# Useless matmuls in the head of an attention and gated-FFN kernel: another operand, another count, other places

## The chip, the cores and the metric

The kernel runs on one core of a Trainium2 chip. The metric is the device time of one execution in microseconds; the time given for a kernel is the median of its runs. A profiled execution gives the page and the trace that the text quotes; all its times count from the start of the core's span. TensorE is called PE there, VectorE DVE, ScalarE ACT, GpSimd POOL and SyncE SP; PEld is TensorE's loading of the stationary operand.

## The reference

Linear attention with a normalised output feeds a feed-forward layer with a sigmoid gate. All is float32 on the chip; the weights of the second part come in as 64-bit floats and are converted by hand.

```python
# q, k, v: (8 batches, 8 heads, 576 tokens, 64)
kv  = einsum('bhsd,bhse->bhde', k, v)
out = einsum('bhsd,bhde->bhse', q, kv)
rms = sqrt(mean(out * out, axis=-1, keepdims=True) + 1e-06)
x   = (out / rms * g_norm)            # then (B*S, H*D) = (4608, 512)
gate = 1 / (1 + exp(-(x @ w_gate)))   # w_gate, w_val: (512, 1536)
val  = x @ w_val
return (gate * val) @ w_out           # w_out: (1536, 512)
```

## The kernel before, in words

The 4608 tokens are taken in nine groups of 512. Group 0 runs through both layers of the feed-forward part in the plain way, 128x512 products at a time (line 618 for the first layer, 853 for the second). The eight other groups use a fast scheme of block products with sums formed ahead of them (lines 977 and 1079), and the attention of the later batches is done in between. All of that follows the head, and the change does not touch it.

The head is the stretch up to about 33 us. It does the attention of batch 0 alone, in four pairs of heads (n = 0 to 3), and converts the first two units of weights. Its order is written out by hand: a string of tokens (`order`, lines 651 to 656), which a loop (lines 658 to 673) turns into instructions one after the other. Each engine works off its own instructions in that order and waits on semaphores where it needs another's result. The tokens are these.

- `KVn` (line 299): 12 small products of k and v on TensorE; `KVOn` (303): VectorE copies the result out.
- `Qn` (309): six transposes of q on TensorE against the identity `ident`; `QOn` (314): ScalarE copies the result out.
- `Un` (326): 20 small products of q and kv; `SQn` (331): ScalarE squares them; `SUMn` (335): VectorE sums the squares; `ROOTn` (339): ScalarE takes the root; `NORMn` (343 and 345): VectorE takes the reciprocal and scales.
- `Xn` (353): five transposes of the scaled result, the second x being `X1`; `XOn` (362): ScalarE copies them into `xT`.
- `cu.i` and `au.i`: the steps of the conversion of weight unit u, the c steps on VectorE (lines 195, 210, 222, 226, 233) and the a steps on ScalarE (200, 215). Step `a0` adds the constant `one` as its bias.
- `b0.i.m` (618): products of the first block of the first layer; TensorE begins the second block after the head, when `c1.4` is done.
- `wu`: loads of weight unit u into a tile `st`.
- `warmN` (671): N products of no use, on the 128x128 tile `ident`, into a PSUM bank that is overwritten later. The profile counts each float32 product as two passes.

Loads of k, v and q for the four pairs go out on SyncE's queue ahead of all this (lines 93 and 100), the weight units in between (159). `ident` is made by GpSimd (a memset and a select in masks.py), and `one`, `exp_off` and `eps` by VectorE memsets (173, 175, 276). Tiles of one pool are placed in SBUF in the order in which they are made, so the size of `one`, the first of them, sets where the others begin.

Of the kernel before, what the change touches and what calls it, by code (L numbers as in the profile page):

```python
# [10 lines left out]
FP32 = mybir.dt.float32  # L11
# [9 lines left out]
def kernel(  # L21
# [11 lines left out]
    nc = tc.nc  # L33
# [4 lines left out]
    P = 128  # L38
# [34 lines left out]
    const = ctx.enter_context(tc.tile_pool(name="const", bufs=1))  # L73
# [75 lines left out]
    def load_unit(u, halves=(0, 1)):  # L149
        if u >= len(units):  # L150
            return
        kind, f = units[u]
        if 0 in halves:
            staged[u] = raw.tile([P, 2, DM], I64, tag="st", name="st", bufs=NST)
        st = staged[u]
        for i in halves:
            if kind == "gv":
                src = (moe_w_gate, moe_w_val)[i].rearrange("(m p) f -> p m f", p=P)[:, :, P * f:P * f + P]
                nc.sync.dma_start(out=st[:, i].rearrange("p (m f) -> p m f", m=NMT), in_=src)
            else:  # L160
                nc.sync.dma_start(out=st[:, i], in_=moe_w_out[P * (f + i):P * (f + i) + P, :])
# [7 lines left out]


    EXP_OFF = 896
    one = const.tile([P, 1], FP32, name="one")
    nc.vector.memset(one, 1.0)
    exp_off = const.tile([P, 1], FP32, name="exp_off")
    nc.vector.memset(exp_off, -EXP_OFF * 2.0 ** 23)

# [83 lines left out]
    w1 = const.tile([P, N3, 4 * NMT, 2, P], FP32, name="w1")  # L260
    w2 = const.tile([P, NFT, DM], FP32, name="w2")
    ident = const.tile([P, P], FP32, name="ident")
# [316 lines left out]
    def bank(i):  # L579
        return (psum_mm if i < 2 else psum).tile([P, 512], FP32, tag=f"mm{i}", name="mm")  # L580
# [19 lines left out]
    warm, pair_kv = bank(0), bank(1)  # L600
# [29 lines left out]
    def plain(c, u, ps, steps_at):  # L630
# [18 lines left out]


    order = """
        w1 w2 warm8 KV0 Q0 KVO0 QO0 warm4 U0 SQ0 KV1 Q1 SUM0 ROOT0 KVO1 QO1 NORM0 warm3 U1 SQ1 X0 XO0 SUM1 ROOT1
        c0.0 a0.0 c0.1 a0.1 NORM1 warm11 X1 XO1 c0.2 KV2 Q2 KVO2 QO2 c0.3 c0.4 w3 warm3 U2 SQ2 KV3 Q3 SUM2 ROOT2 KVO3 QO3
        NORM2 b0.0.0 U3 SQ3 b0.1.0 X2 XO2 c1.0 SUM3 ROOT3 a1.0 c1.1 a1.1 NORM3 b0.0.1 b0.1.1 b0.0.2 X3 XO3 b0.1.2
        c1.2 c1.3 c1.4 w4 b0.0.3 b0.1.3
    """
# [1 line left out]
    for token in order.split():  # L658
        name = token.rstrip("0123456789.")
        n = [int(i) for i in token[len(name):].split(".")]  # L660
        f = n[0]
        if name == "b":
            blk = blk or Plain(0, F_ORDER[0], (warm, pair_kv))
            blk.mm(n[1], n[2])
        elif name in ("c", "a"):
            conversion[f][name][n[1]]()
        elif name == "w":
            load_unit(f)
        elif name == "warm":
            for _ in range(f):  # L670
                nc.tensor.matmul(warm[:, 0:P], ident, ident, start=True, stop=True)
        else:
            a[f][steps[name]]()
            if token == f"Q{NE - 1}":
                first_ctx.__exit__(None, None, None)
                hp = ctx.enter_context(tc.tile_pool(name="hp", bufs=1))
                h_main = [hp.tile([P, 4 * NT, P], FP32, name=f"h{j}") for j in range(N3)]
                h_more = hp.tile([P, N3, 3 * NT, P], FP32, name="h_more")
# [469 lines left out]
    X1 = (18, 19, 20, 21, 22, 22, 23, 23, 24, 24, 25, 26, 28, 30, 31, 33, 35, 37)  # L1148
# [59 lines left out]
```

## Time and profile before

| what | value |
|---|---|
| median of 3 runs | 999.95 us (999.59 to 1000.1) |
| the profiled execution's own time | 1001.39 us |
| its span | 999.6 us |
| TensorE busy | 992.4 us, 99% of the span |
| VectorE, ScalarE, GpSimd busy | 719.1, 343.0, 616.2 us |
| first operation of TensorE | 1.37 us, the first of `warm8` |
| start of KV0, Q0, U0 | 5.08, 6.82, 9.70 us |
| start of U1, X1, U2 | 13.54, 18.38, 21.40 us |

The span runs from the core's first to its last instruction; the execution's own time has what lies around it as well. In the timeline a row names the start, the duration, the engine, the line, the operation, the tiles (out<-in), the shape and the number of instructions, and in brackets the idle time ahead of it and what ended it. In the chain of waits a row is a start, a duration and what the chain went through. Matmuls overlap, so a row's duration is somewhat longer than the distance to the next row's start.

### The profile page before, as it was taken

How to read it: one execution, taken by the hardware profiler on the slowest of the kernel's cores; microseconds unless marked ns; L12 is line 12 of the kernel's file. 1: busy time of each engine (PE TensorE's matmuls, PEld its weight loads, DVE VectorE, ACT ScalarE, POOL GpSimd, SP SyncE). 2: the span in 40 equal slices, each digit the busy share in tenths (PEclk: the TensorE clock that was granted, in tenths of full speed). 3: DMA queues.
4: the chain of work that ended last, by engine and by line, in shares of the span. 5: the costliest groups of instructions: out<-in, count | busy, mean ns of one | idle time of the engine just before them, and what ended most of it. 6: DMA issues, size and time to landing. Idle time of an engine off the chain costs nothing.

```text
span 999.6 us, 16578 instructions
## 1 busy us (share of the span) xinstructions
PE 992.4 (99%) x5958; PEld 816.2 (82%) x5958; DVE 719.1 (72%) x1185; ACT 343.0 (34%) x621; POOL 616.2 (62%) x991
## 2 busy tenths in 40 slices
PE   8999999999999999999999999999999999999998
PEld 7455447888888888888888888888888888888887
DVE  4989999898758766784777576866587566755672
ACT  4566332561144213530344124511442123213320
POOL 0439997798259634865286708771686349744963
PEclk9999999999999999999999999999999999999999
DMA  9995515763889468746975677656854455444614
GB/s 270 275 262 176 174 53 142 220 225 104 289 277 276 158 190 272 205 159 198 280 226 161 187 221 260 176 172 188 282 179 145 152 182 203 158 148 165 215 51 123
DMA packets 149522, 194.96 MB, mean 195 GB/s; under 512 B 79840, under 2 KB 121696, under 8 KB 149440
## 3 DMA queue, kind: packets, MB, share of 16 engines
q0 software_dynamic: 22512, 116.41, 35.1%
q1 hardware_dynamic: 120848, 75.66, 26.7%
q10 hardware_dynamic: 6080, 1.84, 0.8%
q8 instruction: 47, 0.77, 0.3%
q14 instruction: 35, 0.29, 0.1%
HBM read 160.04 MB, written 25.56 MB: 186 GB/s over the span
## 4 chain that ended last, share of the span: by engine, by line
PE 93%; DVE 4%; issue 1%; ACT 1%; DMA 0%; SPq 0%; DVEq 0%; ACTq 0%
PE mm L977 54%; PE mm L1079 27%; PE mm L618 5%; PE mm L853 3%; PE at L450 2%; DVE cz L226 1%; DVE w L222 1%; DVE w L195 1%; PE at L400 1%; PE mm L400 1%; DVE cz L210 0%; DMA q<-in_q_dram 0%; PE two L326 0%; DVE w L235 0%; DVE h L626 0%
## 5 line engine op out<-in xcount | busy, mean ns | idle before, releaser
L977 PE MATMUL mm<-xs,w 128*128 128x256 f32 x1428 | 331.8, 380 | 0.0
L977 PEld LDWEIGHTS mm<-xs,w 128*128 128x128 f32 x1428 | 270.5, 190 | 37.9 <-ACT sg L943 1.2
L977 PE MATMUL mm<-xT,w 128*128 128x256 f32 x948 | 230.6, 380 | 0.0
L977 PEld LDWEIGHTS mm<-xT,w 128*128 128x128 f32 x948 | 179.5, 190 | 25.0 <-issue 0.5
L799 POOL DMA_DIRECT2D w<-kept x84 | 46.9, 559 | 203.6 <-PE mm L977 200.1
L947 DVE TENSOR_TENSOR sg<-sg,mm 128x512 f32<-128x512 f32 (+1 forms) x176 | 100.8, 599 | 75.1 <-PE mm L977 34.4
L1079 PE MATMUL mm<-w,h 128*128 128x256 f32 x630 | 142.8, 379 | 0.0
L1079 PEld LDWEIGHTS mm<-w,h 128*128 128x128 f32 x630 | 119.7, 190 | 16.3
L943 ACT COPY temps<-mm 128x512 f32<-128x512 f32 (+1 forms) x128 | 66.2, 540 | 184.7 <-PE mm L1079 94.7
L939 POOL TENSOR_TENSOR h<-h,sg 128x512 f32<-128x512 f32 x72 | 96.8, 1362 | 43.9 <-ACT sg L936 27.8
L752 POOL TENSOR_TENSOR h<-h 128x128 f32<-128x128 f32 x216 | 109.9, 521 | 16.6 <-DVE h_more L752 13.1
L1079 PE MATMUL mm<-w,h_more 128*128 128x256 f32 x474 | 108.2, 379 | 0.0
L936 ACT ACTIVATE sg<-sg 128x512 f32<-128x512 f32 x96 | 59.7, 630 | 127.3 <-DVE sg L947 127.3
L1079 PEld LDWEIGHTS mm<-w,h_more 128*128 128x128 f32 x474 | 90.1, 190 | 12.2
L943 ACT COPY sg<-mm 128x512 f32<-128x512 f32 (+1 forms) x112 | 56.5, 511 | 84.1 <-PE mm L1079 45.3
L752 POOL TENSOR_TENSOR h_more<-h 128x128 f32<-128x128 f32 x120 | 58.5, 491 | 34.8 <-DVE h L939 30.5
L947 DVE TENSOR_TENSOR temps<-temps,mm 128x512 f32<-128x512 f32 (+1 forms) x96 | 59.5, 620 | 27.1 <-PE mm L1079 16.8
L947 DVE TENSOR_TENSOR temps<-mm,temps 128x512 f32<-128x512 f32 (+1 forms) x64 | 39.8, 623 | 52.3 <-PE mm L1079 23.9
L618 PE MATMUL mm<-xT,w 128*128 128x512 f32 x176 | 77.2, 595 | 0.1
L943 ACT COPY h<-mm 128x512 f32<-128x512 f32 x48 | 28.1, 586 | 142.9 <-PE mm L977 142.9
L947 DVE TENSOR_TENSOR sg<-mm,sg 128x512 f32<-128x512 f32 (+1 forms) x64 | 39.7, 620 | 42.4 <-PE mm L1079 21.9
L618 PEld LDWEIGHTS mm<-xT,w 128*128 128x128 f32 x176 | 32.8, 190 | 40.0 <-issue 36.8
(154 smaller groups left out, 1298.1 us busy)
## 6 DMA issues: line engine op xcount, KB each, us to landing
w<-kept POOLq DMA_DIRECT2D x42, 896.0 KB, 5.1
w<-kept POOLq DMA_DIRECT2D x90, 384.0 KB, 4.5
w<-kept POOLq DMA_DIRECT2D x42, 768.0 KB, 5.0
out_dram<-sg SPq DMA_DIRECT2D x119, 64.0 KB, 1.7
q<-in_q_dram SPq DMA_DIRECT2D x96, 72.0 KB, 5.1
xT<-xTs SPq DMA_DIRECT2D x96, 72.0 KB, 4.6
st<-in_moe_w_gate_dram SPq DMA_DIRECT2D x12, 512.0 KB, 5.3
st<-in_moe_w_val_dram SPq DMA_DIRECT2D x12, 512.0 KB, 6.6
```

The lines of the kernel that those rows point to most:

```text
L400: nc.tensor.matmul(ps[m][HD * g:HD * g + HD, e], mains[2 * m + g, "k"][:, c], mains[2 * m + g, "v"][:, c], start=(b == 2 and e == 0 and j ...
L450: nc.tensor.matmul(to[HD * e:HD * e + HD], qTs[HD * g:HD * g + HD, c:c + HD], kvq[HD * g:HD * g + HD, m, e], start=True, stop=True)
L618: nc.tensor.matmul(self.ps[i], w[("wg", "wv")[i], self.f][:, m, :], xT[self.c][:, m, :], start=(m == 0), stop=(m == NMT - 1), skip_group_c ...
L752: ops.append((eng, lambda v=v, x=x, sign=sign, y=y, eng=eng: eng.tensor_tensor(out=h_form(v, j), in0=h_form(x, j), in1=h_form(y, j), op=op ...
L799: nc.gpsimd.dma_start(out=granule(g)[:, 0:n], in_=kept1[g // NPA % N3, g % NPA][:, 0:n])
L853: nc.tensor.matmul(ps[t], gv[0, f][:, P * t:P * t + P], w["wo", f], start=(f == 0), stop=(f == NFT - 1), skip_group_check=True)
L936: nc.scalar.activation(out=o["o" + step[1]], in_=o["o" + step[1]], func=AF.Sigmoid)
L939: mult.tensor_tensor(out=o[x], in0=o[x], in1=o[y], op=ALU.mult)
L943: nc.scalar.copy(out=o[out_], in_=o[expr])
L947: tt(out=o[out_], in0=o[x], in1=o[y], op=ALU.add if sign == "+" else ALU.subtract)
L977: nc.tensor.matmul(regions[name][1][:, g], ws[:, g], xf[c][wv], start=(new and g == 0), stop=True, skip_group_check=True)
L1079: nc.tensor.matmul(regions[name][1], h_form(hv, j), ws[:, j], start=(used[i] and j == 0), stop=(j == N3 - 1), skip_group_check=True)
```

## The change

A tile of ones, 128x128, takes the place of the 128x1 constant `one`, which becomes its first column; one VectorE memset sets it. The useless products multiply this tile with itself in place of `ident`. Their counts and places change: `warm8` becomes `warm9`; a `warm1` is new between KV0 and Q0; `warm4` ahead of U0 becomes `warm3`; a `warm1` is new between U0 (with SQ0) and KV1; `warm11` ahead of X1 becomes `warm14`. In all that is five products more (from 29 to 34).

```diff
-    one = const.tile([P, 1], FP32, name="one")
-    nc.vector.memset(one, 1.0)
+    ones = const.tile([P, P], FP32, name="ones")
+    nc.vector.memset(ones, 1.0)
+    one = ones[:, 0:1]
...
     order = """
-        w1 w2 warm8 KV0 Q0 KVO0 QO0 warm4 U0 SQ0 KV1 Q1 SUM0 ROOT0 KVO1 QO1 NORM0 warm3 U1 SQ1 X0 XO0 SUM1 ROOT1
-        c0.0 a0.0 c0.1 a0.1 NORM1 warm11 X1 XO1 c0.2 KV2 Q2 KVO2 QO2 c0.3 c0.4 w3 warm3 U2 SQ2 KV3 Q3 SUM2 ROOT2 KVO3 QO3
+        w1 w2 warm9 KV0 warm1 Q0 KVO0 QO0 warm3 U0 SQ0 warm1 KV1 Q1 SUM0 ROOT0 KVO1 QO1 NORM0 warm3 U1 SQ1 X0 XO0 SUM1 ROOT1
+        c0.0 a0.0 c0.1 a0.1 NORM1 warm14 X1 XO1 c0.2 KV2 Q2 KVO2 QO2 c0.3 c0.4 w3 warm3 U2 SQ2 KV3 Q3 SUM2 ROOT2 KVO3 QO3
...
-                nc.tensor.matmul(warm[:, 0:P], ident, ident, start=True, stop=True)
+                nc.tensor.matmul(warm[:, 0:P], ones, ones, start=True, stop=True)
```

## The prediction

> **What bounds the kernel now.** I read the page first, then the chain of waits in order of time, then TensorE's timeline over the head, and last the waits of TensorE after the head.
>
> ```profile
> PE 992.4 (99%) x5958; PEld 816.2 (82%) x5958; DVE 719.1 (72%) x1185; ACT 343.0 (34%) x621; POOL 616.2 (62%) x991
> PE   8999999999999999999999999999999999999998
> ```
>
> TensorE is busy for 99% of the span, and the only slices below 9 are the first and the last. The waits of TensorE from 34 us on hold no row at all. So the end of the run is the end of the head plus a fixed sum of matmuls plus a fixed tail: whatever the head gives up or gains by 33.13 us, when block 1 of the first layer begins, reaches the end unshortened. The question is only how many of the first 33 us the change moves.
>
> The chain of waits, in order of time, shows what sets the head (start, duration, what):
>
> ```profile
> 2.44 4.25 DMA q<-in_q_dram
> 6.68 0.14 issue
> 6.82 1.19 PE two L309 x6
> 8.01 1.76 PE mm L671 x8
> 9.77 1.27 PE two L326 x40
> 11.05 0.02 issue
> 11.07 0.71 ACT sqs L331
> ```
>
> The first q lands at 6.68, its transposes (Q0) follow, then the four useless products of L671 stand on the chain with 1.76 us, then U0. After that the chain alternates between ScalarE, VectorE and TensorE up to the second weight unit's conversion (c1.4), whose last operation ends at 32.98; TensorE begins block 1 at 33.13.
>
> TensorE's own timeline (start, duration, instruction, in brackets the idle time before it):
>
> ```profile
> 1.37 3.78 PE L671 MATMUL mm<-ident 128*128 128x128 f32 x16 [1.37 <-POOL ident masks.py:199]
> 5.08 1.55 PE L299 MATMUL mm<-v,k 96*64 96x64 f32 x24
> 6.82 1.19 PE L309 MATMUL two<-ident,q 96*128 96x96 f32 x6 [0.19 <-DMA q<-in_q_dram]
> 7.80 1.97 PE L671 MATMUL mm<-ident 128*128 128x128 f32 x8
> 9.70 1.29 PE L326 MATMUL two<-kvq,qTs 64*64 64x64 f32 x40
> 10.93 0.92 PE L299 MATMUL mm<-v,k 96*64 96x64 f32 x24
> 11.78 0.71 PE L309 MATMUL two<-ident,q 96*128 96x96 f32 x6
> 13.54 0.81 PE L326 MATMUL two<-kvq,qTs 64*64 64x64 f32 x40 [0.35 <-ACT qTs L314]
> 14.89 2.62 PE L671 MATMUL mm<-ident 128*128 128x128 f32 x22
> 18.38 0.73 PE L353 MATMUL two<-ident,sqs 128*128 128x128 f32 x5 [0.87 <-DVE sqs L345]
> ```
>
> The same work has two prices. A pass of L671 (each product is two passes) costs 3.78/16 = 0.236 us at first and 2.62/22 = 0.119 later; KV costs 1.55 against 0.92, Q 1.19 against 0.71, U 1.29 against 0.81. The page's clock row rounds this away, but the array runs at half rate until some moment inside U0: its first groups still start at the slow distance, its last at the fast one, which puts the rise at about 10.7. TensorE had by then worked since 1.37 with one stop: after KV0, at 6.63, it waits 0.19 us for q. The 5.26 us of unbroken work ahead of that stop did not raise the clock; the 3.9 us after it did.
>
> [...]
>
> **The change, part by part.** TensorE gets two rows more (850 to 852); no other engine's order changes, nor any DMA's.
>
> Start. The operand is now `ones`, one VectorE memset at 0.81, where before two GpSimd operations ended at 1.31. VectorE's memset of 128x1 takes 0.06 and GpSimd's of 128x128 takes 0.20; so `ones` is ready between 0.87 and 1.01, TensorE follows 0.05 later, and begins 0.30 to 0.45 us sooner. I take 0.35, near the 128x128 row. The two small memsets behind it on VectorE slip by up to 0.15, and their readers come far later (ScalarE's first activation at 3.29).
>
> warm9. One product more: 2 x 0.236 = 0.47. KV0 starts at 5.08 - 0.35 + 0.47 = 5.20 (its v has landed at 4.82) and ends at 6.75.
>
> The first new warm1 takes 0.47, so Q0 starts at about 7.2, not 6.82. That is +0.4 on the chain, and TensorE no longer stops there. warm3 in place of warm4 gives 0.47 back. With the slow clock all through: Q0 to about 8.2, three products (6 x 0.236 = 1.4) to 9.6, U0 at 9.6 against 9.70: a gain of 0.1, no more.
>
> The second warm1 costs 2 x 0.119 = 0.24 ahead of KV1. It is hidden: Q1 ends at 12.49 and ScalarE copies it only at 12.87, behind ROOT0, so 0.38 us of cover. Without that cover it would cost 0.24.
>
> warm14. Three products more, 6 x 0.119 = 0.71, in the 0.87 us in which TensorE waits for VectorE's NORM1 ahead of the second x: hidden with 0.16 to spare. Uncovered it would cost up to 0.7.
>
> What the filled wait does to the clock is shown by no row of before, so I bound it. Lower end: nothing, the gain of 0.1. Upper end: the clock is up before Q0. Then Q0 waits for its data (6.82 as now) and takes 0.6 of TensorE's time, not 1.0; ScalarE copies it 0.25 after that for 0.64, and U0 starts at 8.3, not 9.70 (1.4 sooner), taking 0.81, not 1.29 (0.5): 1.9 in all. Between them: TensorE now works unbroken from about 1.02, so 5.26 us of it are over at 6.3 and the rise should come somewhere from there on. With a rise during Q0 (7.2 to 7.8) Q0 ends at 7.8, the copy at 8.7, U0 starts 1.0 sooner and takes 0.5 less: 1.5.
>
> What is late next: after U0 the chain is engine on engine, so 1.5 is passed on until the second weight unit's data, which land at 23.95. Its first conversion step (c1.0) starts at 25.26 now, so this can move by 1.2 at most; the steps behind it wait for ScalarE and move by the full 1.5, and the gap closes to some 0.1 to 0.2. Everything else in the head (q2 at 17.56, v3 at 19.68, q3 at 20.49) lands before its moved use. I take 1.35.
>
> The sum against the profiled execution: it took 1001.39 (span 999.6 and 1.8 around it), and 1001.39 - 1.35 = 1000.04. The timed runs have a median of 999.95, 1.44 below the profiled one. If that is what profiling costs, the changed kernel takes 999.95 - 1.35 = 998.6; bounds 998.05 (1.9) and 999.85 (0.1).
>
> Addresses. `one` was 4 bytes per partition and `ones` is 512, so nearly every tile allocated after it moves up by 480 bytes: q, k, v, h and xT, which began on multiples of 256 bytes, begin 224 past one. I cost that at nothing. On TensorE, L977's passes lie 216 ns apart with xT as with the weight ring, which already begins 224 past; on the queues, the weight units' packets of 1024 bytes, written into `st`, which begins 224 past, take 46 ns, in line with the 18 ns of a 256-byte packet into the aligned q tiles.
>
> **The rivals.**
>
> First, the timed runs already have the early rise. The 1.44 us by which they beat the profiled run is about what the early rise is worth (1.35 to 1.9). If the moment of the rise depends on where the first matmul falls, the profiled run was the unlucky one, and the change has 0 to 0.3 left to give: 999.8. For it: 1.44 fits; against it: three runs within 0.5 us of each other, and profiling may well cost this much. [...]
>
> Second, the change doesn't do what it says: the stop of 0.19 us is not what held the clock. Q0's six transposes, 1.0 us at the slow rate, lay across the same place, and stay there. Then the rise stays at about 10.7 and the result is -0.1 to +0.3: 1000.0. [...]
>
> Third, slower: the shifted addresses split packets. In the head the DMA engines are the pace (busy share 0.9 and above from 3 to 30 us). If each of the 4608 q packets (256 bytes) and 1536 k and v packets of the head pays a second packet's fixed cost of some 9 ns (a packet of 128 bytes takes 13 ns and one of 256 takes 18, which leaves 8 or 9 for one without data), that is 6144 x 9 / 16 = 3.5 us more ahead of the second weight unit. It lands at 27.4 in place of 23.95, c1.0 starts 2.2 later, and the run takes 1002.2. It decides from 1.3 us of added DMA time on, the slack of c1.0 today. Against it: the 46 ns above, at the same offset. [...] The `st` rows do not agree with a visible cost.
>
> Fourth, more than forecast: if the timed runs rise even later than the profiled one, after 14 us, U0, KV1, Q1 and U1 all ran slow, about 1.1 us more than in the profile, and the change brings 1.9 + 1.1 = 3.0: 997.0. For it speaks only the narrow spread of the timed runs.
>
> **How the numbers follow.** A measurement of this kernel can tell about 0.2%, that is 2.0 us, from no change. Forecast (rise before or in Q0, against timed runs that rise late): 0.42, at 998.6, of which 0.10 lies beyond 2.0 us, since its upper end of 1.9 is worked from rounded rows. Timed runs already early: 0.30, at 999.8. Rise unmoved: 0.13, at 1000.0. Packets split, or another delay of that size: 0.07, at 1002.2. A still later rise in the timed runs: 0.08, at 997.0. So faster by over 0.2%: 0.10 + 0.08 = 0.18; slower: 0.07; within: 0.75. The range 997.9 to 1000.3 takes in the first three cases but for the edge of the forecast, and leaves out the last two: about 8 in 10.
>
> **What would show it.** In the profile after: L671 starting near 1.0; no idle bracket at Q0 (L309); Q0 at about 7.2 with later passes at the fast distance; U0 at 8.7 or sooner and at 0.81 us, not 1.29; the second x still waiting for VectorE, with a wait of 0.1 to 0.3, not 0.87; block 1 at about 31.8, not 33.13; and a span near 998.2. The forecast is wrong if U0 stays near 9.6 at 1.29 us, if the second x waits for TensorE's own products, or if q or the weight units land later than now.

## The result: 6 us slower, and what the profile after shows

| | changed kernel | kernel before |
|---|---|---|
| median of the timed runs | 1006.08 us (1005.14 to 1008.99, 6 runs) | 1000.03 us |
| ratio | 1.0062, 95% interval 1.005 to 1.0074 | 1 |
| the profiled execution's own time, span | 1006.25, 1004.5 us | 1001.39, 999.6 us |

The forecast was 998.6 us, with a range up to 1000.3. One of the six runs of the kernel before took 3718.28 us; the ratio goes by the others. A second measurement of the changed kernel, on record as a0_after_again, gave 1007.07 us, ratio 1.0066 (1.0051 to 1.0081).

The page of the changed kernel, busy time of each engine and TensorE's row in 40 slices:

```profile
PE 993.4 (99%) x5968; PEld 816.2 (81%) x5968; DVE 718.1 (71%) x1185; ACT 343.0 (34%) x621; POOL 614.8 (61%) x991
PE   9989999999999999999999999999999999999998
```

TensorE has ten passes more and 1.0 us more busy time, but the span is 4.9 us longer: the loss is waiting. The new 8 is the third slice, about 50 to 75 us, far behind the last instruction that the diff touches.

TensorE's timeline over the head of the changed kernel (start, duration, instruction, in brackets the idle time before it):

```profile
1.06 4.21 PE L672 MATMUL mm<-ones 128*128 128x128 f32 x18 [1.06 <-DVE eps L277]
5.20 1.55 PE L300 MATMUL mm<-v,k 96*64 96x64 f32 x24
6.68 0.71 PE L672 MATMUL mm<-ones 128*128 128x128 f32 x2
7.22 0.66 PE L310 MATMUL two<-ident,q 96*128 96x96 f32 x6
7.72 0.86 PE L672 MATMUL mm<-ones 128*128 128x128 f32 x6
8.61 0.81 PE L327 MATMUL two<-kvq,qTs 64*64 64x64 f32 x40
13.41 3.29 PE L672 MATMUL mm<-ones 128*128 128x128 f32 x28
16.90 0.74 PE L354 MATMUL two<-ident,sqs 128*128 128x128 f32 x5 [0.20 <-DVE sqs L346]
22.22 0.69 PE L310 MATMUL two<-ident,q 96*128 96x96 f32 x6 [0.63 <-DMA q<-in_q_dram]
```

What the forecast said of the first half of the head is there: the start at 1.06, Q0 at 7.22 without a wait and at the fast rate, U0 at 8.61 and 0.81 us long, the second x waiting only 0.20. The clock rose at 7.17 (10.81 before), and X1 starts 1.48 us sooner. From there on the gain shrinks: Q3 waits 0.63 for q, and block 1 begins at 32.23, 0.90 sooner than before and not 1.35. The first conversion step of the second weight unit (c1.0), on VectorE, shows where that went; the first line is the changed kernel, the second the kernel before:

```profile
25.28 0.69 DVE L196 TENSOR_SCALAR w<-st 128x1024 uint32<-128x1024 uint32 x1 [1.41 <-DMA st<-in_moe_w_val_dram]
25.25 0.77 DVE L195 TENSOR_SCALAR w<-st 128x1024 uint32<-128x1024 uint32 x1
```

The step waits 1.41 us for its weights, and starts no sooner than before. The chain of waits of the changed kernel, in order of time (start, duration, what), goes through transfers where before it went from engine to engine (an excerpt):

```profile
6.24 7.28 DMA st<-in_moe_w_val_dram
13.51 0.02 issue
13.53 8.55 DMA q<-in_q_dram
22.08 0.14 issue
22.22 0.69 PE two L310 x6
```

Behind the head no wait of TensorE over 0.15 us stood in the trace before. The waits of TensorE of the changed kernel from 33 us on (engine, line, what ended the waits: us in total, times, longest):

```profile
PE mm L978 <- issue: 2.0, 2, 1.5
PE at L451 <- ACT kvq L414: 1.6, 1, 1.6
PE mm L619 <- issue: 1.1, 1, 1.1
PE mm L854 <- DVE w L236: 0.4, 2, 0.2
```

They are of two kinds: waits for data that hang on a load, and waits put down to "issue", where TensorE waited for nothing that the profile shows. The DMA issues of both pages (tile, kernel, queue, count, size, median us from issue to landing) show the loads. Before:

```profile
q<-in_q_dram SPq DMA_DIRECT2D x96, 72.0 KB, 5.1
st<-in_moe_w_gate_dram SPq DMA_DIRECT2D x12, 512.0 KB, 5.3
st<-in_moe_w_val_dram SPq DMA_DIRECT2D x12, 512.0 KB, 6.6
```

After:

```profile
q<-in_q_dram SPq DMA_DIRECT2D x96, 72.0 KB, 6.0
st<-in_moe_w_gate_dram SPq DMA_DIRECT2D x12, 512.0 KB, 7.3
st<-in_moe_w_val_dram SPq DMA_DIRECT2D x12, 512.0 KB, 7.6
```

The bytes and the packets are the same. In the packet records of the first 24 us, a 256-byte packet into q takes 23.4 ns on the mean (18.8 before) and one of 1536 bytes into k and v 93.7 (84.7). These are the tiles that begin 224 bytes past a multiple of 256 since the tile of ones grew. The first difference is clear of what varies between runs: the kernels below whose q tiles are aligned have 18.6 to 19.7, those with shifted ones 23.4 to 25.4. For the 1536-byte packets the spans come close, 84.7 to 90.7 against 92.5 to 102.8.

### The profile page after: what moved, and what is told of

Its sections match the earlier page's. It is cut to its first block, busy times and chain, and to the rows that moved or that the text cites. A ratio compares the mean times of both kernels' runs of the same rounds, so it can differ in the third digit from the quotient of the medians.

```text
span 1004.5 us, 16598 instructions
## 1 busy us (share of the span) xinstructions
PE 993.4 (99%) x5968; PEld 816.2 (81%) x5968; DVE 718.1 (71%) x1185; ACT 343.0 (34%) x621; POOL 614.8 (61%) x991
## 4 chain that ended last, share of the span: by engine, by line
PE 89%; DVE 5%; DMA 3%; issue 1%; SPq 1%; ACT 0%; DVEq 0%
PE mm L978 54%; PE mm L1080 27%; PE mm L854 3%; PE mm L619 2%; PE at L451 2%; DMA st<-in_moe_w_val_dram 1%; DVE cz L227 1%; DVE w L223 1%; DMA q<-in_q_dram 1%; DMA h_more<-in_v_dram 1%; DVE w L196 1%; SPq L132 1%; PE at L401 1%; PE mm L401 1%; DVE cz L211 0%
## 5 line engine op out<-in xcount | busy, mean ns | idle before, releaser
L978 PE MATMUL mm<-xs,w 128*128 128x256 f32 x1428 | 331.9, 380 | 1.5 <-issue 1.5
L978 PEld LDWEIGHTS mm<-xs,w 128*128 128x128 f32 x1428 | 270.5, 190 | 39.6 <-issue 1.7
L978 PE MATMUL mm<-xT,w 128*128 128x256 f32 x948 | 230.8, 380 | 0.5 <-issue 0.5
L978 PEld LDWEIGHTS mm<-xT,w 128*128 128x128 f32 x948 | 179.5, 190 | 25.7 <-issue 1.2
```

What stands on the lines that cost most here:

```text
L978: nc.tensor.matmul(regions[name][1][:, g], ws[:, g], xf[c][wv], start=(new and g == 0), stop=True, skip_group_check=True)
```

## The experiments

Two numbers of each trace order all runs: the start of block 1, which ends the head, and the time from there to TensorE's last instruction, which before was 995.73 - 33.13 = 962.60 us. "Added" counts TensorE's instructions against before: the five products more are 20, as each is two passes and each pass a weight load and a product.

| kernel | big tiles past a multiple of 256 B | added | median us | ratio (95%) | block 1 | from block 1 on |
|---|---|---|---|---|---|---|
| before | 0 | 0 | 1000.03 | 1 | 33.13 | 962.60 |
| changed | 224 | 20 | 1006.08 | 1.0062 (1.005, 1.0074) | 32.23 | 968.35 |
| a0_after_again | 224 | 20 | 1007.07 | 1.0066 (1.0051, 1.0081) | 33.87 | 967.20 |
| e1_after_512 | 0 | 20 | 1000.77 | 1.0006 (0.9997, 1.0015) | 31.31 | 964.79 |
| e2_before_480 | 224 | 0 | 1002.11 | 1.0016 (1.0007, 1.0025) | 33.68 | 963.67 |
| e5_order_alone | 0 | 20 | 1000.29 | 0.9999 (0.999, 1.0008) | 31.64 | 963.22 |
| e4_first_h_aligned | 0 where loads of k, v, q, h land; others 224 | 20 | 1000.98 | 1.0006 (0.9997, 1.0015) | 31.91 | 964.59 |
| e6_512_warm9 | 0 | 0 | 1000.10 | 0.9999 (0.9987, 1.0011) | 31.52 | 962.60 |
| e9_512_h_off | 0, but h 224 | 20 | 1004.66 | 1.0046 (1.0028, 1.0063) | 31.69 | 965.74 |
| e10_480_h_on | 224, but h 0 | 20 | 1002.74 | 1.0019 (1.001, 1.0029) | 36.63 | 963.19 |
| e7_off64 | 64 | 20 | 1005.70 | 1.0044 (1.003, 1.0057) | 32.28 | 967.52 |
| e11_all_256 | 0, `st` too | 0 | 999.54 | 0.9986 (0.9977, 0.9994) | 31.27 | 962.58 |
| e12_before_warm16 | 0 | 20 | 1001.39 | 1.0003 (0.9994, 1.0012) | 33.16 | 963.12 |
| e13_480_warm9 | 224 | 0 | 1001.87 | 1.002 (1.0011, 1.0029) | 32.21 | 963.60 |
| e14_before_all_256 | 0, `st` too | 0 | 999.67 | 0.9998 (0.9989, 1.0006) | 31.37 | 962.06 |

Each ratio is to runs of the kernel before on the same chip, and not to the 1000.03 of the first row; e1, e2, e4 and e5 shared theirs, as did a0, e6, e9 and e10, then e7, e11 and e12, then e13 and e14. e2, e12 and e14 have the order of before; all others have the new order (e6, e11 and e13 with nine products ahead of the second x), and of these e5 starts at 1.37 as before, since it keeps the identity tile. The two columns on the right are of one profiled execution each.

### Order or addresses

e1_after_512, the changed kernel with the tile of ones 32 bytes larger, so that all later tiles stand on multiples of 256 again:

```diff
-    ones = const.tile([P, P], FP32, name="ones")
+    ones = const.tile([P, P + 8], FP32, name="ones")[:, 0:P]
```

> The changed kernel, with the tile of ones 544 bytes long per partition in place of 512 (the products still read its first 128 columns). Every later tile then lies 512 bytes above its place in the kernel before, not 480, so q, k, v, h and xT begin on multiples of 256 again; the order and the products are those of the changed kernel. Address theory (packets that begin off a 256-byte boundary take longer, and the loads of the head and of h_more come late): the loss of 6 us goes and the earlier clock stays, 0.9 to 1.9 us under the kernel before, 998.1 to 999.1. Timing theory (the earlier head makes the SyncE and GpSimd loads collide, whatever the addresses): about 1006. In the trace the 256-byte packets of the head average 18.8 ns by the address theory, 23 by the other.

e2_before_480, the kernel before with the 512-byte tile alone:

```diff
-    one = const.tile([P, 1], FP32, name="one")
+    one = const.tile([P, P], FP32, name="one")[:, 0:1]
```

> The kernel before, with the tile `one` 512 bytes long per partition; only its first column is set and used. Order and products are those of before, all later tiles move up by 480 bytes. Address theory: the packets slow down as in the changed kernel (256-byte ones from 18.8 to 23 ns on average), q3 lands after 21.5 in place of 20.5, TensorE stops for h_more near 60 us, and the run takes 1004 to 1008. Timing theory: no change, 999.6 to 1000.3.

e5_order_alone, the kernel before with the new `order` string and nothing else:

> Only the new counts and places of the useless products, still on the identity and at the old addresses, so they begin at 1.37 as before. [...] Timing theory: slower, 1003 to 1006, as far as the head still ends sooner.

e4_first_h_aligned, the changed kernel with 32 bytes more ahead of the tiles that k, v, q and the later tiles of the pool `hp` (h and `h_more`) are loaded into; `xT`, `xTs` and the late q tiles stay at 224:

```diff
+    sb.tile([P, 8], FP32, name="pad", bufs=1)
```

> The changed kernel with 32 bytes of padding behind the tiles that live through the whole kernel, so that the head's k, v, q and the later h and h_more begin on multiples of 256 again, while xT, xTs and the late q tile stay 224 past one. Address theory: if the loads of the head and of h_more make the loss near 60 us, that stop goes and q3 lands near 20.5; what the late q loads (128-byte packets) and the writes to xT lose stays, 999 to 1004. If all of the loss is in the head and h_more: 998.5 to 999.5. Timing theory: about 1006.

Thirty-two bytes of padding take back all but some 0.6 of the 6 us (e1), and so does aligning only the tiles that loads of the head and of batch 1 go into (e4). The new order alone costs nothing that can be told from no change (e5). The gain of 0.9 to 1.9 us that was expected of e1, and of 0.5 to 1.5 of e5, did not come. So the address does it, but not alone: with the order of before the same shift costs 1.6 us (e2), a quarter of the loss and not the 4 to 8 us that were expected.

a0_after_again, the changed kernel once more beside the runs that follow:

> The changed kernel itself once more, on the chip of the parts, so that they can be compared with it. Both theories: 1005 to 1007, with the stop of about 2 us ahead of the head's successor near 61 us and stops of 0.7 and 1.6 us near 506 and 719.

It gave 1007.07 us, with the waits at the same places (1.2 us for `kvq`, stops of 1.3 and 1.1 us; the one near 720 us is 0.1). Its profiled execution spreads the loss otherwise than the first: the clock is up at 5.16, but Q0, Q1 and Q3 wait 0.55, 0.67 and 0.46 us for q and the second x 1.34, and block 1 begins at 33.87, later than before.

### What the five added products have to do with it

In the profile after, the waits put down to "issue" end at 64.63, 506.17 and 719.62 us. Counted through the trace, these are TensorE's instructions number 1217, 6593 and 9409 (weight loads, products and semaphore instructions together, counted from 0), all of them 193 more than a multiple of 256. One of the DMA queues that the page calls "instruction" moves packets of 16 KB, one of which starts 2.4 us ahead of each stop's end: at 62.24, 503.72 and 717.21. The page has 47 packets in that queue, and the trace 12203 instructions of TensorE, 260 to a packet; the stops lie 5376 = 21 x 256 and 2816 = 11 x 256 instructions apart. From these numbers it is estimated that a packet brings a block of 256 of TensorE's instructions; no record names what a packet holds.

e6_512_warm9 is e1 with nine products in the last changed place and not fourteen, so that TensorE issues as many instructions as before:

```diff
-        c0.0 a0.0 c0.1 a0.1 NORM1 warm14 X1 XO1 ...
+        c0.0 a0.0 c0.1 a0.1 NORM1 warm9 X1 XO1 ...
```

> The changed kernel at aligned addresses (tile of ones 544 bytes), and with nine useless products ahead of the second x in place of fourteen, so that TensorE has as many instructions in the head as the kernel before. Theory of instruction fetch (the stops near 503 and 715 us fall on the same TensorE instructions, 6593 and 9409, whatever the time, 11 x 256 apart; they are blocks of instructions that arrive late): the block ends return to where they lie in the kernel before, and the two stops, 0.27 and 0.51 us, go: 0.3 to 0.8 under the aligned kernel with fourteen, 999.8 to 1000.4. Rival (the stops are waits for data that the earlier head brings about): they stay at the same work. In both, the second x waits 0.6 us longer on TensorE without a loss, as VectorE ends that wait.

No stop was left at any of the three, and from 33 us on TensorE has no wait over 0.15 us. From block 1 to the end it took 962.60 us, the same as before to the hundredth. e1 stops at all three, for about 0.9, 0.3 and 0.5 us. (These and the parts below are the distances between the starts of neighbouring products, less the same distances in e6; the idle times of the views are somewhat shorter.)

e13_480_warm9 makes the same edit, nine products for fourteen ahead of the second x, in the changed kernel itself, with its shifted addresses:

> The changed kernel with its 480-byte ones tile kept (every later tile 224 bytes past a multiple of 256) and nine products in the first group instead of fourteen, so that TensorE issues no more instructions than the kernel before. Theory one (the 6 us are late loads plus late blocks of TensorE's instructions): the stops at TensorE's instructions 1217, 6593 and 9409 go, with about 1.2, 0.7 and 1.6 us of their own, and 1002.5 to 1004 us is left. Theory two (the addresses alone make the whole loss): about 1006 us, with stops at the same places or waits for data instead. Theory three (the blocks alone, the addresses cost nothing without them): within 0.7 us of the kernel before.

It took 1001.87 us, 2.0 more than before, a little under the first theory's span and outside the others. One wait of TensorE is left behind the head (view as above):

```profile
PE at L451 <- ACT kvq L414: 1.0, 1, 1.0
```

So the addresses and the added instructions together cost more than the sum of the two. From block 1 on, against 962.60: shifted addresses alone +1.0 (e13) and +1.1 (e2); twenty instructions alone +0.5 (e12), +0.6 (e5) and +2.2 (e1); both +5.75 and +4.6 (the changed kernel, twice), where the largest sum is 3.3. Each is from one profiled execution.

The place where they meet is at 56 to 65 us, where VectorE and ScalarE convert a weight unit and ScalarE copies `kvq` for batch 1. In e6 (timeline):

```profile
55.85 0.68 DVE L196 TENSOR_SCALAR w<-st 128x1024 uint32<-128x1024 uint32 x1
59.06 0.27 ACT L414 COPY kvq<-at 128x128 f32<-128x128 f32 x1 [0.30 <-PE at L401]
59.85 1.21 PE L451 MATMUL at<-kvq,qTs 64*64 64x64 f32 x66
```

In the changed kernel:

```profile
59.10 0.69 DVE L196 TENSOR_SCALAR w<-st 128x1024 uint32<-128x1024 uint32 x1 [1.89 <-DMA st<-in_moe_w_val_dram]
59.83 1.15 ACT L201 ACTIVATE w<-w,ones 128x1024 f32<-128x1024 uint32 x1 [5.42 <-DVE w L196]
61.92 0.24 ACT L414 COPY kvq<-at 128x128 f32<-128x128 f32 x1
62.22 1.21 PE L451 MATMUL at<-kvq,qTs 64*64 64x64 f32 x66 [1.59 <-ACT kvq L414]
64.63 1.55 PE L619 MATMUL mm<-xT,w 128*128 128x512 f32 x3 [1.14 <-issue]
```

The weights land late, the conversion step starts 3.25 us later (0.71 of it is the head), ScalarE has its own step (L201) in front when the product of k and v is ready, and copies it behind that; TensorE waits for the copy. What makes the weights late stands in the chain of the changed kernel (start, duration, what; an excerpt):

```profile
41.31 3.25 SPq L132
44.56 0.04 issue
44.60 7.86 DMA h_more<-in_v_dram
52.47 0.02 issue
52.48 6.52 DMA st<-in_moe_w_val_dram
```

Lines 132 and 137 issue the loads of k and v into `h_more`, which is shifted, on SyncE's queue, and the weights' loads stand behind them there. The issues for `h_more` run from 37.31 to 51.35 us, against 36.60 to 45.73 in e6, and the first load of weights behind them goes out at 51.59 against 45.83.

Behind U of batch 1 (L451) lies, by the estimate above, the end of a block: its last product is instruction 1216, at 63.28, and instruction 1217 starts at 64.63, 2.39 us after the start of a packet. In kernels with the order's old count instruction 1217 lies 20 instructions further on in the work; in the kernel before it starts at 66.63, 0.43 us after the weight load ahead of it (66.20), and TensorE does not stop there.

By these traces the 5.75 us that the changed kernel loses from block 1 on against e6 are: the wait ahead of U of batch 1, 1.66; instruction 1217, 1.20; waits for weights that VectorE converts, at 118 to 126 us, 0.57; instruction 6593, 0.69; instruction 9409, 1.64; sum 5.76. In the head it gives up 0.71 more. In the second profile (a0) the same parts are 1.30, 1.34, 0.45, 1.25 and 0.27, and the head gives up 2.35. In e13 the first is 1.05 and the others are gone. In the aligned e1 the packets start 2.35 to 2.54 us ahead of the ends of the stops, much as here; so a stop was longer where its packet started later. The one for instruction 1217 starts at 59.23 in e1 and at 62.24 here, 0.02 us after TensorE has resumed from its wait for the copy. Why it starts later is not shown.

### Which tiles, which offset

e9_512_h_off is e1 with a pad of 224 bytes at the start of `hp`, so that only `h` and `h_more` are shifted:

```diff
                 hp = ctx.enter_context(tc.tile_pool(name="hp", bufs=1))
+                hp.tile([P, 56], FP32, name="pad")
```

> The changed kernel at aligned addresses, but with h and h_more alone moved to begin 224 bytes past a multiple of 256 (224 bytes of padding ahead of them). Theory that the loss near 60 us is the loads into h_more and h (k, v and the first late q) taking longer: the stop of 2 us returns and the run takes 1002 to 1004, with the head ending as early as in the aligned kernel. Rival, that it is the head's own loads of q, k and v being late: no change from the aligned kernel, 1000 to 1001.

e10_480_h_on is the changed kernel with 32 bytes there, so that only `h` and `h_more` are aligned:

```diff
                 hp = ctx.enter_context(tc.tile_pool(name="hp", bufs=1))
+                hp.tile([P, 8], FP32, name="pad")
```

> The changed kernel with 32 bytes of padding ahead of h and h_more, so that these alone begin on multiples of 256 and the head's q, k, v, as well as xT and the late q, stay 224 past one. Theory that the loads into h and h_more make the loss: most of it goes, 1001 to 1003; q3 still lands late, after 21.5, and block 1 begins near 32.2. Rival, that the head's own loads make it: 1004 to 1006.

With the `hp` tiles alone shifted (e9) the run is 0.0046 longer, some 4.6 us and a little over what was expected; of that 0.6 is e1's own. Its profiled run (1003.15, the fastest of the six) shows one large wait from 33 us on, at instruction 1217:

```profile
PE mm L619 <- issue: 1.8, 1, 1.8
```

With only the other tiles shifted, 1.9 us are lost (e10). The two parts add up to about the whole: 4.0 + 1.3 + 0.6 = 5.9. e10's profiled execution says little about its other runs: it took 1005.49 against a median of 1002.74, and its clock rose only at 17.31 (Q0 at 7.98, after a wait of 0.36 for q).

e7_off64 is the changed kernel with the tiles 64 bytes past a multiple of 256:

```diff
-    ones = const.tile([P, P], FP32, name="ones")
+    ones = const.tile([P, 152], FP32, name="ones")[:, 0:P]
```

> The changed kernel with the tile of ones 576 + 32 bytes long per partition, so that every later tile that was at 224 past a multiple of 256 is 64 past one. If what counts is that a packet crosses a 256-byte boundary, the 256-byte packets of q cross one as before and average 22 to 24 ns in the head, and the run takes 1004 to 1007. If what counts is a start off a multiple of 64, they average 18.5 to 19.5 and the run takes 1000.5 to 1001.5.

64 past costs most of what 224 past does (1.0044 against 1.0062 and 1.0066; from block 1 on 967.52 us against 968.35 and 967.20), and 256-byte packets take 23.6 ns there. So a start on a multiple of 64 was not enough; of the three offsets tried, only 0 was free of the cost. In these runs it is the written side of the loads that is shifted, and their 256-byte packets take 23.4 to 25.4 ns in place of 18.6 to 19.7; why they take longer is not shown.

### The clock, the count alone, and a version with everything aligned

b1_before_look, the kernel before, for one more profile:

> The kernel before, one look. Its timed runs fall in two groups, 999.2 to 1000.2 and 1001.0 to 1002.4; the first profile was of the upper one. If the groups are the two moments of the clock's rise, a run of the lower group shows U0 and Q0 at the fast rate and block 1 near 31.3; a run of the upper group shows U0 at 1.29 us as in the first profile.

Its time was 1001.25, and the clock rose in time and fell again (timeline of TensorE, then the busy time of the engines in two stretches, whose last three figures are the granted clock, the DMA share and GB/s; what lies ahead of the first clock record, at 4.29, counts there as granted in full):

```profile
4.89 0.92 PE L299 MATMUL mm<-v,k 96*64 96x64 f32 x24
7.13 0.69 PE L309 MATMUL two<-ident,q 96*128 96x96 f32 x6 [1.32 <-DMA q<-in_q_dram]
7.65 1.91 PE L671 MATMUL mm<-ident 128*128 128x128 f32 x8
9.50 1.35 PE L326 MATMUL two<-kvq,qTs 64*64 64x64 f32 x40
```

```profile
3.60:7.20 3.60, 2.19 (x33) 1.91 (x32) 0.22 (x1) 0.00 (x0) 0.00 (x0) 1.00 0.96 274
7.20:11.00 3.80, 3.80 (x58) 3.46 (x60) 0.00 (x0) 0.73 (x2) 0.00 (x0) 0.57 1.12 297
```

KV0 ran at 0.92 us, the fast price, then Q0 waited 1.32 us for q, and the eight passes of L671 were back at the slow price. The clock's records stand at 4.29 (up), 7.70 (down) and 11.11 (up), 3.41 apart. Shorter stops at the same place did not take the clock back: 0.78 us in e2 and 0.55 in a0 and e14.

The runs of the kernel before fall into two groups, most clearly those beside a0, where 12 of 23 lie at 1000.1 or below and 11 at 1001.26 or above. Both profiles of before (1001.39 and 1001.25) belong to the upper group, and both had the slow clock at U0. That the lower group are runs with the early rise is inferred from that and from e14 below, which has the order of before, rose at 4.93 and took 999.14; a profile of the kernel before in the lower group was not met.

Over all profiles, the clock was up for good by 7.29 us in ten of the eleven with the new order (e10 is the other), and in two of the five with the order of before (e2 at 5.31, e14 at 4.93). Whether it is the stop ahead of Q0 that holds it is not shown. In e12 that stop is only 0.07 us long, and the clock rises at 10.87 all the same. In e10 TensorE stops for nothing from 7.98 to 17.31, and the clock is slow throughout. Where the rise came at 6.26 to 7.29 us with the new order, it came before Q0's transposes or within 0.02 us of their start, so these runs cannot tell the filled stop from the second rival, which has Q0's six transposes across the same place.

e12_before_warm16, the kernel before with sixteen products in place of eleven ahead of the second x: the count of the changed kernel, nothing else.

```diff
-        c0.0 a0.0 c0.1 a0.1 NORM1 warm11 X1 XO1 ...
+        c0.0 a0.0 c0.1 a0.1 NORM1 warm16 X1 XO1 ...
```

> The kernel before, at its own addresses and with its identity operand, with 16 useless products ahead of the second x in place of 11: as many TensorE instructions in the head as in the changed kernel, nothing else. Theory of instruction fetch: stops of 0.3 to 1 us return at TensorE's instructions 1217 (near 64 us), 6593 (near 504) or 9409 (near 716), and the run takes 1000.8 to 1002, of which up to 0.3 is the second x waiting for TensorE. Rival (the stops come from the earlier head): 1000.1 to 1000.4.

Its interval (0.9994 to 1.0012) settles nothing. Its profile shows stops at instruction 1217, of 0.14 us, and at 9409, of 0.27.

e11_all_256 is the order of e6 with padding that puts `st`, the weight tiles and the sums on multiples of 256 too, which before they were not (three smaller pads are left out here):

```diff
-    ones = const.tile([P, P], FP32, name="ones")
+    ones = const.tile([P, P + 24], FP32, name="ones")[:, 0:P]
...
+            raw.tile([P, 56], FP32, name="pad")
...
+            sums.tile([P, 56], FP32, name="pad2")
```

> The aligned kernel with nine products ahead of the second x, and with padding that puts nearly every other tile on a multiple of 256 bytes too: the weight units' tile st, the weights w1 and w2, the sums xs, the store tiles sg, which lay 192, 224 or 32 past one in the kernel before. If the place in the 256 bytes costs all transfers, the packets of the weight units (1024 bytes) get shorter in the head (before: 54.5 ns on average up to 24 us), the weights land sooner, and the run is 0.3 to 1.5 us under the kernel with nine products: 998.6 to 999.8. If only small packets pay, or only starts off 64 bytes, nothing changes: 1000.

e14_before_all_256 has the same padding under the order of before, with the products on the identity tile:

> The kernel before, with its order and its products on the identity tile, and padding that puts nearly all tiles on multiples of 256 bytes. If the gain of the aligned variant of the changed kernel (0.9986 of the time before) comes from the addresses alone: 0.9980 to 0.9992. If it needs the changed order with its earlier rise of the clock: 0.9992 to 1.0005, with the same two kinds of runs as the kernel before.

Against the runs beside it e11 is 1.4 us faster than the kernel before (ratio 0.9986, 0.9977 to 0.9994), and its median is 6.5 below the changed one's. Those runs of before had a median of 1000.87, though, with 11 of 21 above 1000.6; beside e14 the kernel before had 999.75, with 6 of 21 there, and e14 at 999.67 is the same as it. The packets of the weights are shorter with `st` aligned (1024-byte packets 50.7 ns in e11's head, 51.0 in e14's, 54.5 before), but whether e11 beats before by more than that draw of runs, and whether its order or its addresses do it, these runs leave open.

## Why the prediction was wrong, step by step

**Start, warm9, the warm1 tokens, warm14: right.** The first product began at 1.06 (forecast near 1.0), KV0 at 5.20 (5.20), Q0 at 7.22 (7.2), and the second x waits 0.20 (0.16 spare).

**The filled wait and the clock: it came out as forecast, but the cause is not shown.** The rise came at 7.17, Q0 was fast, U0 began at 8.61. That the filled stop did it, and not where Q0's transposes fall, no run tells (e12 and e10 above speak against the stop as the whole reason). Aligned and with the old count (e6) block 1 begins at 31.52, 1.61 sooner than in the first profile and a little beyond the 1.35 forecast, and the profiled execution takes 1.56 less than that of before.

**"If that is what profiling costs": wrong, as far as the times tell.** The 1.44 us between the profiled run and the timed ones was most likely the first rival's: by their times, over half of the timed runs already had the early rise. e6 has 1000.10 against 1000.10 for the kernel before. With aligned addresses the changed order took 1000.77 (e1), so had the addresses cost nothing, the rival's 999.8 would have been nearer than 998.6.

**"Addresses ... I cost that at nothing": this is the step that failed.** The evidence for it was a packet of 1024 bytes into `st`, 224 past a boundary, at 46 ns. That is the commonest value; the mean in the head is 54.5, and 50.7 with `st` aligned (e11). In place of nothing, the shifted addresses cost 1.6 us by themselves (e2) and some 5.5 of the 6 us together with the 20 instructions (the changed kernel against e1). The third rival had longer packets in the head, at a chance of 0.07; that packets are split, as it says, no run shows, only that they take longer (23.4 ns in place of 18.8 for 256 bytes, 93.7 in place of 84.7 for 1536). Its size in the head, 3.5 us of DMA time, came from 9 ns for every packet; on the mean a 256-byte packet pays 4.6 and a 1536-byte one 9.0, which is (4608 x 4.6 + 1536 x 9.0) / 16 = 2.2 us. At block 1 it was 0.7 us in two profiles (the changed kernel and e13, against e6) and 2.35 in a third (a0), where the rival had 2.2. What the rival did not have at all is the rest, from block 1 on.

**"Reaches the end unshortened": right for a head that ends sooner and wrong as it was used.** With the old instruction count and aligned addresses the stretch from block 1 on is 962.60, 962.60 and 962.58 us (before, e6, b1), whenever block 1 begins. But that no wait stands in the trace of before was read as room without end. The load of the weights that are converted at 56 us had less to spare than the shift took, and the ends of TensorE's instruction blocks, as estimated above, none that could be seen. The edit changed both: the loads into the tiles that moved and those queued behind them, through the address, and the place of every block's end, through 20 more instructions. "The end of the head plus a fixed sum" was therefore wrong by 4.6 to 5.75 us. "No other engine's order changes, nor any DMA's" was true, but the transfers' durations changed.

## What to carry to other kernels

A first tile of a pool that grows by a size that is no multiple of 256 bytes moves the tiles behind it off their boundary: here 256-byte packets took 23.4 ns on the mean at 224 past it, 23.6 at 64 past it (e7) and 18.8 on it. Look at where the loads land before costing an edit to such a tile, and pad it. A row of waits that is empty says that nothing is late now, not how much may become late; look for the slack of the loads behind the edit. Where instructions are added to an engine that is busy all the time, pads and counts have to be tried together, since 1 us and some 0.5 to 2 us of loss by themselves made 4.6 to 5.75 together here.

## What the runs showed of the hardware that had not been expected

- A load whose tile begins 64 or 224 bytes past a multiple of 256 has packets of two kinds: of 4608 packets of 256 bytes, 4113 took 18 to 20 ns and 271 took 24 to 45 when aligned (before), 2341 and 1961 when shifted (after).
- TensorE's own pace was the same at both addresses: passes of L977 (L978 or L979 where lines were added) mostly lie 216 ns apart, before and after, in shifted and aligned kernels.
- With 20 instructions more, TensorE stopped at its instructions 1217, 6593 and 9409, for 1.20, 0.69 and 1.64 us in the changed kernel; at 1217 from 0.14 us (e12) to 1.8 (e9). About 2.4 us went by from the start of a 16 KB packet of the instruction queue to the first instruction behind the stop (2.39, 2.45, 2.41 in the changed kernel).
- A clock once granted was taken back within the head where TensorE had stopped for 1.32 us (b1), and given again 3.41 us later; a stop of 0.78 us at the same place (e2) did not take it back.
